# Windowed attention with an FFN behind it: global scores in the banks of the value products, and the second batch's attention in 32-query blocks

## The chip, the cores and the metric

The kernel runs on one core of one Trainium2 chip. The metric is the time of one execution on the device in microseconds (us). Every time comes from runs on the chip; the profile is that of one execution.

## The reference

Eight batches with eight heads of 64 dimensions. Each head has 512 local and 32 global tokens. A local query sees the 32 global keys and the local keys within 32 positions of it; a global query sees all 544 keys. The outputs of the heads, side by side, are the rows of x (4352 x 512), which go through an FFN:

```python
s_g = scale * q_g @ concat(k_g, k_l).T          # global queries, all keys
s_ll = where(abs(i - j) <= 32, scale * q_l @ k_l.T, -1e9)
out_l = softmax(concat(scale * q_l @ k_g.T, s_ll)) @ concat(v_g, v_l)
h = x @ w_in                                    # 512 -> 2048
out = (h - tanh(h)) @ w_out                     # 2048 -> 512
```

## The kernel before

**FFN.** x, the weights and g = h - tanh(h) are each split into a high and a low part in fp32r, and a product is three matmuls (high x high, low x high, high x low). The matmuls of the hidden layer are in line L1186, those of the output in L1234; 336 of 128x512 belong to each batch's local tokens. The 256 global tokens of all batches go through the FFN at the end (L1560 and after). The weights come as float64 and are converted on chip in 40 pieces (24 wide, 16 half). DVE takes part in all of them (L440, L444), ACT, POOL and DVE share the split into high and low (L367, L450).

**Attention.** Heads go in pairs, four pairs to a batch, 32 in all. Pairs 0 to 7 (batches 0 and 1) are of class `Pair`: 128-query tiles, in which PE turns K and Q (L544), makes scores (L640, global L577, L578), turns the probabilities (L660, L615) and multiplies with V (L737). Pairs 8 to 31 are of class `WindowPair`: 32-query blocks, in which DVE turns K and Q as they come from memory (L846, L853) and the probabilities (L1012, 16 per pair), so that PE has only scores (L873), global scores (L894) and value products (L1042). DVE takes the peaks of the rows (L972, global L906) and moves small statistics between partitions (L913, L919, which POOL may do too). The results leave a product's bank in two steps, x_hi (a cast on ACT or DVE, L367) and x_lo with the global rows xg (DVE).

**Visits.** PE's work for window pairs is grouped into visits between the FFN matmuls: both products of pair j and the scores of pair j+1 are one visit (a joint visit here); the global scores of pair j+1 are a visit of their own some FFN matmuls later, in two PSUM banks of their own. Banks 0 to 3 serve attention and the hidden layer by turns, 4 to 7 the FFN output.

**Order.** Each step is handed to a planner (`Order`) with the engines that can do it, a due time (worked out from the table `CFG`) and the data and banks that it needs. The planner lays out all engines' work in time and emits each engine's instructions in that order; each engine runs them strictly in this order. Where it expects PE to idle in the first 72 us, it puts in filler matmuls (L1842). SP issues nearly all loads, in the planned order.

Of the kernel before, what the change touches and what calls it, by code (L numbers as in the profile page):

```python
# [8 lines left out]
F32 = mybir.dt.float32  # L9
# [7 lines left out]
P = 128  # L17
D = 64
W = 32
KC = 224  # L20
KG = 352
# [186 lines left out]
def kernel(ctx, tc, q_l, k_l, v_l, q_g, k_g, v_g, w_in, w_out, out):  # L208
# [3 lines left out]
    NT = S // P  # L212
# [21 lines left out]
    wraw = [wpair[:, :256], wpair[:, 256:], cp.tile([P, 256, 2], F32, name="wraw2", tag="wraw2")]  # L234
# [19 lines left out]
    first_raw = [first_raw[:, 0], first_raw[:, 1], rawkq.rearrange("p (a t h d) -> p a t h d", a=2, t=NT, h=2)]  # L254
    first_kw = cp.tile([P, 2, 2 * S], F32, name="first_kw", tag="x_lo1")
    first_kw = [first_kw[:, 0, :2 * KG], first_kw[:, 1, :2 * KG], first_kw2]
    first_q = cp.tile([P, 4 * DM], F32, name="first_q", tag="w_out_lo4")
    wide = [wpair, first_q[:, 2 * DM:].rearrange("p (n k) -> p n k", k=2), stage[:, 0], stage[:, 1]]
    first_q = [first_q[:, :S], first_q[:, S:2 * S], cp.tile([P, S], F32, name="first_q2", tag="hi0")]
# [5 lines left out]
    SETS = [[f"{n}{u}" for n in ("rk", "rq", "pw", "pk", "pq")] for u in range(2)] + [["raw", "kq", "kw0", "kg0", "hk0"]]  # L265
# [50 lines left out]
    def bank(shape, j, dt=F32):  # L316
# [6 lines left out]
        elif len(shape) == 4:  # L323
# [4 lines left out]
    CFG = dict(win=-466.5653, a_g=1.5262, a_kg=1.4158, a_ph=0.7742, a_qs=2.9873, a_w=0.3174, a_wn=0.0, a_xg=7.3446, d_g=1.972,  # L328
               d_gl=1.6793, d_kg=0.2625, d_kq=0.1607, d_ph=0.0221, d_pl=3.1864, d_qh=27.4739, d_qs=0.035, d_tg=1.1442, d_tp=0.8276,
               d_w=0.5897, d_wl=0.2437, d_wn=2.2842, d_xg=1.1595, d_y=0.042, gfirst=0.0, ho=5649.5935, hs=-43.0719, lag=-64.2863,  # L330
               last=-56.3309, o_st0=-2045.5745, o_st1=933.0264, o_tw0=-2840.8346, o_tw1=5048.3316, one=0.0, p0=190.4904, pen=23.1854,
               penp=47.4685, s_g=0.5, s_gl=20.2886, s_kq=73.0039, s_p=1.9417, s_tg=0.5596, s_w=7.2868, s_wl=12.2887, step=129.7289,
               step1=9.9947, lag0=83.3228, hs0=44.3799, tol=0.0776, xs=0.0373, xw=3.2349, o_ld0=-276.9069, o_tn0=1314.6887,
               o_sg0=1087.8972, o_tg0=246.2107, o_s0=671.959, o_sp0=362.8471, o_t0=283.5775, o_tpp0=1378.7205, o_vl0=2890.1138,
               o_vl1=-609.1368, o_pv0=2012.3724, o_pvp0=8038.7725, o_ld1=4474.6221, o_pv1=5749.1756, o_pvp1=-4996.466,
# [433 lines left out]
    def add_window_masks():  # L769
# [24 lines left out]
        for j in range(NT):  # L794
            add(("P", 1.2), mask(j), due + j, w=["gm"], res=[("wraw", 2), "ga", "gb"] if j == 0 else ())
# [532 lines left out]
    def attention(j):  # L1328
# [3 lines left out]
        if j + 1 == H // 2:  # L1332
            add_first_globals(1)
# [545 lines left out]
```

## Time and profile before

| | us |
|---|---|
| median of 3 runs | 927.95 (927.31 to 928.08) |
| profiled execution | 928.72 |
| its span in the trace | 926.9 |
| PE busy | 912.6 |
| DVE busy | 695.1 |
| ACT busy | 393.7 |
| POOL busy | 345.4 |

The span is the time from the first to the last instruction in the trace; 1.8 us of the profiled execution lie outside it. The execution has four stages. In the start (to 60 us) batch 0's attention runs and the first weights are converted. Then batch 0's FFN runs with batch 1's attention and the other weights, to the first window visit. Then follow the FFN of batches 1 to 7 with the window pairs of the next batch between, to 796 us, and the global tokens' FFN at the end. In the trace's rows a number behind a name's line is the start, then the duration; "x4" is four instructions in a row.

### The profile page before, as it was taken

The numbers are of one execution on the slowest core, as the hardware profiler recorded it, in microseconds if no ns is written. First come the engines' busy times: TensorE is split into PE (matmuls) and PEld (weight loads), VectorE is DVE, ScalarE is ACT, GpSimd is POOL, SyncE is SP. The second block draws the span as 40 slices with busy tenths as digits, with TensorE's granted clock in tenths as the row PEclk, the third lists the DMA queues.
The fourth block names the chain that finished last, engine by engine and source line by source line (L and its number), as shares of the span: only waits on it lengthen the run. The fifth ranks groups of instructions, "written<-read, shape, count | busy, mean of one in ns | idle before, by whom it ended". The sixth has DMA issues, their size and how long they took to land.

```text
span 926.9 us, 21769 instructions
## 1 busy us (share of the span) xinstructions
PE 912.6 (98%) x7838; PEld 744.7 (80%) x7838; DVE 695.1 (75%) x2244; ACT 393.7 (42%) x1145; POOL 345.4 (37%) x588
## 2 busy tenths in 40 slices
PE   7899999999999999999999999999999999999998
PEld 5677877878888888888888888888888888898986
DVE  6887757488888896868876986778776968868773
ACT  6966666434334442433334332433334342433232
POOL 3667765633432434333332443434343432110000
PEclk9989999999999999999999999999999999999999
DMA  9555343333234332332413332432322320100001
GB/s 234 137 159 180 116 136 95 82 85 64 58 76 115 65 74 52 87 82 59 80 42 83 76 68 39 109 63 58 76 57 81 73 46 1 46 1 1 0 1 69
DMA packets 248172, 70.12 MB, mean 76 GB/s; under 512 B 232704, under 2 KB 241408, under 8 KB 248064
## 3 DMA queue, kind: packets, MB, share of 16 engines
q1 hardware_dynamic: 246720, 68.21, 31.7%
q8 instruction: 62, 1.02, 0.5%
q10 hardware_dynamic: 1344, 0.52, 0.2%
q14 instruction: 46, 0.38, 0.1%
HBM read 59.77 MB, written 8.91 MB: 74 GB/s over the span
## 4 chain that ended last, share of the span: by engine, by line
PE 94%; DVE 2%; DMA 2%; POOL 1%; ACT 0%; issue 0%; SPq 0%; ACTq 0%; DVEq 0%; POOLq 0%
PE bank L1234 34%; PE bank L1186 33%; PE bank L1560 7%; PE bank L1680 6%; PE bank L1042 5%; PE bank L873 3%; PE bank L640 1%; PE bank L894 1%; PE bank L737 1%; PE bank L1586 1%; DMA rawkq<-in_k_l_dram 1%; PE bank L660 1%; PE bank L544 1%; DMA first_raw<-in_q_l_dram 0%; DMA wpair<-in_moe_w_out_dram 0%
## 5 line engine op out<-in xcount | busy, mean ns | idle before, releaser
L1203 POOL TENSOR_TENSOR glo<-t,ghi 128x512 fp32r<-128x512 f32 x112 | 145.2, 1297 | 310.1 <-PE bank L1234 201.3
L1012 DVE STREAM_TRANSPOSE keys_first<-prob 32x256 f32<-32x256 f32 x384 | 167.4, 436 | 21.9 <-POOL prob L994 15.6
L1194 ACT ACTIVATE t<-bank 128x512 f32<-128x512 f32 x112 | 66.9, 597 | 201.1 <-PE bank L1186 197.9
L1197 DVE TENSOR_TENSOR t<-bank,t 128x512 f32<-128x512 f32 x112 | 77.2, 689 | 74.2 <-ACT t L1194 72.7
L1234 PE MATMUL bank<-w_out_hi,glo 128*128 128x512 f32 x448 | 125.5, 394 | 0.0
L1234 PE MATMUL bank<-w_out_lo,ghi 128*128 128x512 f32 x448 | 124.7, 392 | 0.0
L1234 PE MATMUL bank<-w_out_hi,ghi 128*128 128x512 f32 x448 | 124.5, 392 | 0.0
L1186 PE MATMUL bank<-x_hi,w_in_hi 128*128 128x512 f32 x448 | 123.3, 397 | 0.3 <-DVE x_hi L367 0.3
L1186 PE MATMUL bank<-x_hi,w_in_lo 128*128 128x512 f32 x448 | 120.3, 391 | 0.0
L1186 PE MATMUL bank<-x_lo,w_in_hi 128*128 128x512 f32 x448 | 120.3, 390 | 0.0
L1186 PEld LDWEIGHTS bank<-x_hi,w_in_hi 128*128 128x128 f32 x448 | 82.2, 188 | 21.4 <-DVE xg L1077 2.0
L1186 PEld LDWEIGHTS bank<-x_lo,w_in_hi 128*128 128x128 f32 x448 | 84.0, 188 | 18.1 <-issue 0.2
L1186 PEld LDWEIGHTS bank<-x_hi,w_in_lo 128*128 128x128 f32 x448 | 83.8, 188 | 18.0 <-issue 0.2
L1234 PEld LDWEIGHTS bank<-w_out_lo,ghi 128*128 128x128 f32 x448 | 83.2, 188 | 18.6 <-issue 0.7
L1234 PEld LDWEIGHTS bank<-w_out_hi,glo 128*128 128x128 f32 x448 | 82.8, 188 | 19.1 <-issue 1.5
L1234 PEld LDWEIGHTS bank<-w_out_hi,ghi 128*128 128x128 f32 x448 | 83.3, 188 | 18.2 <-issue 0.5
L994 POOL TENSOR_SCALAR prob<-prob,st 128x128 f32<-128x128 f32 x192 | 67.7, 372 | 56.6 <-DVE st L987 56.6
L367 ACT CAST ghi<-t 128x512 fp32r<-128x512 f32 (+1 forms) x76 | 46.5, 612 | 98.4 <-PE bank L1234 81.1
L980 ACT ACTIVATE prob<-prob,st 128x128 f32<-128x128 f32 x192 | 74.6, 391 | 3.1 <-DVE st L972 3.0
L1042 PEld LDWEIGHTS bank<-keys_first,values 128*64 128x64 f32 x672 | 42.2, 138 | 8.5 <-DVE t L1197 2.8
L1042 PE MATMUL bank<-keys_first 128*64 128x32 f32 (+2 forms) x672 | 46.8, 228 | 0.0
L1042 PE MATMUL bank<-keys_first,values 128*64 128x32 f32 (+2 forms) x672 | 46.8, 228 | 0.0
(252 smaller groups left out, 1476.3 us busy)
## 6 DMA issues: line engine op xcount, KB each, us to landing
out_dram<-wpair SPq DMA_DIRECT2D x28, 256.0 KB, 2.1
rawkq<-in_q_l_dram SPq DMA_DIRECT2D x96, 64.0 KB, 2.3
rawkq<-in_k_l_dram SPq DMA_DIRECT2D x96, 64.0 KB, 2.3
stage<-in_moe_w_out_dram SPq DMA_DIRECT2D x6, 512.0 KB, 3.9
wpair<-in_moe_w_out_dram SPq DMA_DIRECT2D x6, 512.0 KB, 4.3
first_q<-in_moe_w_in_dram SPq DMA_DIRECT2D x6, 512.0 KB, 4.0
stage<-in_moe_w_in_dram SPq DMA_DIRECT2D x6, 512.0 KB, 3.7
values<-in_v_l_dram SPq DMA_DIRECT2D x24, 120.0 KB, 2.3
```

The costliest lines, as they stand in the source:

```text
L367: (nc.scalar.copy if e == "A" else nc.vector.tensor_copy)(dst, src)
L980: nc.scalar.activation(x, x, AF.Exp, bias=s[:, k:k + 1], scale=-1.0, accum_out=s[:, 8 + k:9 + k])
L994: nc.gpsimd.tensor_scalar(x, x, s[:, k:k + 1], 1.0, op0=ALU.mult, op1=ALU.mult)
L1012: nc.vector.transpose(view(win_kf[W * k:W * k + W], [(CH, 2), (P, NT), (1, W)], 3 * G + W * i), src)
L1042: nc.tensor.matmul(dst, win_values[h][:, window(b)], src, start=n == 0, stop=n == len(parts) - 1, skip_group_check=True)
L1186: nc.tensor.matmul(self.h[s][:, j * n:(j + 1) * n], w[:, cc, f * P:(f + 1) * P], self.x()[xi][:, cc, :n], start=part == 0 and cc == 0 and ...
L1194: nc.scalar.activation(tt_[q], self.h[s], AF.Tanh)
L1197: nc.vector.tensor_sub(tt_[q], self.h.pop(s), tt_[q])
L1203: eng[e].tensor_sub(gg[q][1], tt_[q], f32(gg[q][0]))
L1234: nc.tensor.matmul(self.acc[tt], g[:, j * self.n + tt * P:j * self.n + (tt + 1) * P], low_out(f) if wi else high_out(f), start=s == 0 and ...
L1560: nc.tensor.matmul(self.hold(tt, tags), g(), low_out(f) if wi else high_out(f), start=first and k < len(tts), stop=last and k == len(mms) - 1)
L1680: nc.tensor.matmul(dst[:, at], w, m, start=fresh and n == 1, stop=n == 6, skip_group_check=True)
```

## The change

Three things and a new table:

- Only pairs 0 to 3 are of class `Pair`; pairs 4 to 7 are window pairs like the later ones. The window masks and the loads for them come earlier (`add_window_masks` is due at batch 1).
- The global scores of pair j+1 are glued to the joint visit, behind its local scores. They have no banks of their own: they are written into columns 288 and up of the two banks that hold the products of pair j, which come free once both the product's x_lo and the global peak have read them. The first window pair's global scores still get two banks, in the visit of its scores.
- A weight buffer (`wraw[2]`) becomes a view of one that is needed for first-pair global keys; the third sets of load buffers for pairs 4 to 7 go.
- All numbers of `CFG` are new, so that the planner lays out all engines anew.

Line numbers are 1 to 2 higher after the change (L873 is L874, L894 L896, L1012 L1014, L1042 L1044, L1186 L1188, L1234 L1236); the fillers are L1839.

```diff
-    wraw = [wpair[:, :256], wpair[:, 256:], cp.tile([P, 256, 2], F32, name="wraw2", tag="wraw2")]
+    wraw = [wpair[:, :256], wpair[:, 256:], first_kw2[:, :512].rearrange("p (n k) -> p n k", k=2)]
...
-    CFG = dict(win=-466.5653, a_g=1.5262, a_kg=1.4158, a_ph=0.7742, a_qs=2.9873, a_w=0.3174, a_wn=0.0, a_xg=7.3446, d_g=1.972,
+    CFG = dict(win=-386.7662, a_g=0.1365, a_kg=4.903, a_ph=0.7671, a_qs=2.6529, a_w=0.057, a_wn=0.2074, a_xg=0.0096, d_g=0.1819,
...
-        due = base(2 * H) - 300
+        due = base(H) - 300
...
-        def global_scores(self):
+        def global_scores(self, before=None):
             names = [("sg", self.j, h) for h in range(2)]
+            self.gtoks = names if before is None else [("o", before.j, h) for h in range(2)]
...
-                t_ = self.box["g"] = [bank([P, NG_], tags[n]) for n in names]
+                t_ = self.box["g"] = [bank([P, 288 + NG_], tags[n])[:, 288:] for n in self.gtoks]
...
-                add(("D", 0.45), peak(h), due(1.5), r=[("sg", self.j, h), "gm"], w=[key(h), (st, h)], free=[(("sg", self.j, h), 1)])
+                add(("D", 0.45), peak(h), due(1.5), r=[("sg", self.j, h), "gm"], w=[key(h), (st, h)], free=[(self.gtoks[h], 1 + (self.gtoks[h][0] == "o"))])
...
-            own = [n for x in parts for n in x["names"]]
+            own = [n for x in parts for n in x["names"] if x.get("own", True)]
...
-                w=[k + (1,) for k in x] + [("xg", 2 * self.j, half), ("xg", 2 * self.j + 1, half), ("xgw", 2 * self.j)], free=[(o, 1)])
+                w=[k + (1,) for k in x] + [("xg", 2 * self.j, half), ("xg", 2 * self.j + 1, half), ("xgw", 2 * self.j)], free=[(o, 1 + (self.j + 1 < len(pairs)))])
...
-    pairs = [(Pair if j < H else WindowPair)(j) for j in range(NH // 2)]
+    pairs = [(Pair if j < H // 2 else WindowPair)(j) for j in range(NH // 2)]
...
-        if j == H:
+        if j == H // 2:
             add_window_masks()
             add_globals(p.b)
             p.add_load()
-            p.add_visit(p.at, [p.scores()])
-        p.add_visit(p.after(1.0), [p.global_scores()])
+            p.add_visit(p.at, [p.scores(), p.global_scores()])
...
-        p.add_visit(p.after(16.0), [p.product(0), p.product(1)] + ([other.scores()] if other else []))
+        p.add_visit(p.after(16.0), [p.product(0), p.product(1)] + ([other.scores(), other.global_scores(p)] if other else []))
...
-            (attention if i < 2 * H else window_attention)(i // 2)
+            (attention if i < H else window_attention)(i // 2)
```

**How the order changes.** First PE, around the global scores of a window pair. A row names the bank written, then the weights and the moving operand. Before, they stand alone between FFN output matmuls, in two banks that nothing else uses at that time:

```order
L1234 MATMUL bank_102<-w_out_hi,ghi_72 128x512
L1234 MATMUL bank_103<-w_out_hi,ghi_72 128x512
L894 MATMUL bank_99<-first_m,win_gq 32x2x64
L894 MATMUL bank_98<-first_m,win_gq 32x2x64
...
L894 MATMUL bank_98<-first_m,win_gq 32x64
L1234 MATMUL bank_104<-w_out_lo,ghi_72 128x512
```

After, they follow the local scores of the same visit, and bank_96 is the one that the second product has just filled:

```order
L1044 MATMUL bank_96<-keys_first,values 64x96
L1044 MATMUL bank_96<-keys_first 64x96
L874 MATMUL bank_98<-first_m,hi_104 32x128
L874 MATMUL bank_99<-first_m,hi_104 32x128
...
L896 MATMUL bank_97<-first_m,win_gq 32x2x64
L896 MATMUL bank_96<-first_m,win_gq 32x2x64
...
L896 MATMUL bank_96<-first_m,win_gq 32x64
L1188 MATMUL bank_98<-x_hi_105,w_in_hi 128x512 x4
```

What moved: one visit instead of two, and the global scores now stand behind the readers of the products' banks. FFN matmuls between joint visits are 92 mostly, as the kernel before had 96; in front of the first four joint visits they are 72, 120, 108 and 84.

Second, DVE around the last x_lo of batch 0 (which the first FFN matmuls wait for) after the change. Names: `first_m` and `hi` are turned K and Q of a window pair, `st` the statistics, `stage`, `wpair` and `first_q` weight buffers:

```order
L988 TENSOR_SCALAR st_91<-st_91 128x4
L989 RECIPROCAL st_91<-st_91 128x4
L847 STREAM_TRANSPOSE first_m<-rawkq 128x5x96
L848 STREAM_TRANSPOSE first_m<-rawkq 128x32
L854 STREAM_TRANSPOSE hi_104<-rawkq 128x512
L368 CAST x_hi_85<-bank_100 128x256
...
L445 SCALAR_TENSOR_TENSOR first_q<-first_q 128x512
L921 COPY st_91<-st_91 32x2 x3
L749 TENSOR_TENSOR x_lo_86<-bank_100,x_hi_85 128x256
L753 COPY xg<-bank_100 128x32
L749 TENSOR_TENSOR x_lo_86<-bank_102,x_hi_85 128x256
```

What moved: the first window pair's softmax and the second one's turns now stand ahead of the last x_lo of batch 0, where before only weight pieces and rows of `Pair` stood. On PE, 73 fillers (before 18) stand between the last product of batch 0 and the first FFN matmul.

Third, the first rows of SP, which issue the first pairs' loads. Before:

```order
L528 DMA first_raw_81<-in_k_l_dram 128x4x64
L528 DMA first_raw_81<-in_q_l_dram 128x4x64
L483 DMA wraw2_67<-in_k_g_dram 32x8x64
L483 DMA wraw2_67<-in_q_g_dram 32x8x64
L1146 DMA values_86<-in_v_l_dram 96x3x64 x2
L1148 DMA values_86<-in_v_g_dram 32x6x64
```

After:

```order
L529 DMA first_raw_80<-in_k_l_dram 128x4x64
L1148 DMA values_84<-in_v_l_dram 96x3x64 x2
L1150 DMA values_84<-in_v_g_dram 32x6x64
L529 DMA first_raw_80<-in_q_l_dram 128x4x64
L484 DMA first_kw2_63<-in_k_g_dram 32x8x64
L484 DMA first_kw2_63<-in_q_g_dram 32x8x64
```

What moved: the three loads of V stand ahead of the first Q.

## Rows read from the trace of the kernel before

**Rows 1.** The page: busy us, share of the span and instructions of each engine.

```profile
PE 912.6 (98%) x7838; PEld 744.7 (80%) x7838; DVE 695.1 (75%) x2244; ACT 393.7 (42%) x1145; POOL 345.4 (37%) x588
```

**Rows 2.** What PE waited for: us in total, times, longest.

```profile
PE bank L544 <- DMA first_raw<-in_k_l_dram: 4.1, 1, 4.1
```

**Rows 3.** Stretches: start:end, length, busy PE, PEld, DVE, ACT, POOL, clock, DMA, GB/s.

```profile
10.00:40.00 30.00, 28.05 (x299) 20.06 (x295) 27.61 (x118) 27.15 (x93) 15.63 (x29) 1.00 0.83 211
30.00:40.00 10.00, 9.41 (x103) 6.41 (x102) 9.46 (x42) 8.96 (x31) 4.89 (x10) 1.00 0.70 184
...
10.01:187.52 177.51, 172.03 (x1269) 132.45 (x1266) 127.43 (x396) 119.85 (x335) 110.70 (x165) 0.98 0.53 142
...
187.52:796.22 608.70, 608.70 (x5917) 495.53 (x5917) 477.54 (x1675) 226.61 (x724) 222.07 (x395) 1.00 0.31 67
200.00:300.00 100.00, 100.00 (x1086) 81.40 (x1086) 85.43 (x304) 38.72 (x123) 36.36 (x70) 1.00 0.34 71
```

**Rows 4.** Timeline of PE, start of the FFN: start, us, engine, line, operation.

```profile
60.18 0.94 PE L1186 MATMUL bank<-x_hi,w_in_hi 128*128 128x512 f32 x3
61.39 0.47 PE L1186 MATMUL bank<-x_hi,w_in_hi 128*128 128x512 f32 x1 [0.27 <-DVE x_hi L367]
```

**Rows 5.** Timeline of PE, first window visit, scores and global scores together.

```profile
187.52 1.13 PE L873 MATMUL bank<-first_m,hi 64*32 64x128 f32 x63 [0.73 <-DVE first_m L847]
...
188.96 1.20 PE L1234 MATMUL bank<-w_out_hi,ghi 128*128 128x512 f32 x4
```

**Rows 6.** Timeline of PE, a joint visit and the global scores behind it.

```profile
400.21 0.30 PE L1042 MATMUL bank<-keys_first,values 128*64 128x96 f32 x1
...
402.09 1.16 PE L873 MATMUL bank<-first_m,hi 64*32 64x128 f32 x64
403.18 0.50 PE L1234 MATMUL bank<-w_out_hi,glo 128*128 128x512 f32 x1
...
407.89 1.07 PE L1186 MATMUL bank<-x_hi,w_in_lo 128*128 128x512 f32 x4
408.88 0.56 PE L894 MATMUL bank<-first_m,win_gq 64*32 64x128 f32 x32
409.38 1.20 PE L1234 MATMUL bank<-w_out_hi,glo 128*128 128x512 f32 x4
410.41 0.85 PE L1234 MATMUL bank<-w_out_hi,ghi 128*128 128x512 f32 x3
```

**Rows 7.** Timeline of PE, 72 FFN matmuls without a visit, to the global tokens' FFN.

```profile
779.90 1.07 PE L1186 MATMUL bank<-x_hi,w_in_hi 128*128 128x512 f32 x4
...
796.22 1.07 PE L1586 MATMUL bank<-x_hi,w_in_hi 128*128 128x512 f32 x4
```

**Rows 8.** Groups of DVE instructions by shape: count, busy us, mean ns, idle before.

```profile
L1012 DVE STREAM_TRANSPOSE keys_first<-prob 32x256 f32<-32x256 f32 x384 | 167.4, 436 | 21.9 <-POOL prob L994 15.6
L919 DVE COPY st<-st 32x2 f32<-32x2 f32 x138 | 26.1, 189 | 2.8
L853 DVE STREAM_TRANSPOSE hi<-rawkq 128x512 f32<-128x512 f32 x24 | 16.6, 691 | 0.8 <-PE bank L640 0.8
L444 DVE SCALAR_TENSOR_TENSOR stage<-stage 128x512 int32<-128x512 int32 x12 | 10.0, 836 | 0.4
L444 DVE SCALAR_TENSOR_TENSOR wpair<-wpair 128x512 int32<-128x512 int32 x6 | 7.0, 1174 | 0.2
```

**Rows 9.** Timeline of DVE: the first softmax, the last x_hi and x_lo of batch 0.

```profile
10.01 0.39 DVE L1124 CUSTOM_DVE_ANT_0 t<-bank,mask 128x224 f32<-128x224 f32 x1 [1.95 <-PE bank L640]
...
60.83 0.41 DVE L367 CAST x_hi<-bank 128x256 fp32r<-128x256 f32 x1
61.28 0.42 DVE L748 TENSOR_TENSOR x_lo<-bank,x_hi 128x256 fp32r<-128x256 f32 x1
61.62 0.20 DVE L750 TENSOR_TENSOR xg<-bank,xg 128x32 f32<-128x32 f32 x1
```

**Rows 10.** Timeline of SP's queue: the first loads of V.

```profile
2.81 0.96 SPq L1146 DMA_DIRECT2D values<-in_v_l_dram  x2
```

More of the change, by code (lines that the diff above doesn't have):

```diff
@@ L791, in ends @@
                 nc.vector.memset(win_gmask()[W * rows:W * rows + W, W * lo:W * hi], BIG)
-        due = base(2 * H) - 300
+        due = base(H) - 300
         for j in range(NT):
-            add(("P", 1.2), mask(j), due + j, w=["gm"], res=[("wraw", 2), "ga", "gb"] if j == 0 else ())
+            add(("P", 1.2), mask(j), due + j, w=["gm"], )
         add(("D", 0.5), ends, due, w=["gm"])
@@ L813, in add_globals @@
         add(("S", 4.4), load, due, w=["raw"], xfer=0.73)
-        add(("D", 0.56), turn, due + 64.0, r=["raw"], w=[("gkq", b % 2)], res=["fm", "gl0"] if b == 2 else [])
+        add(("D", 0.56), turn, due + 64.0, r=["raw"], w=[("gkq", b % 2)], res=["fm", "gl0"] if b == 1 else [])
     class WindowPair:
@@ L824, in __init__ @@
             self.prob, self.box = win_p, {}
-            self.over = ["h00", "h01", "h10", "h11", "hg0", "hg1"] if j == H else []
+            self.over = ["h00", "h01", "h10", "h11", "hg0", "hg1"] if j == H // 2 else []
         def after(self, us):
@@ L856, in add_load @@
                 add(("S", 2.2), load(a, src), self.after(-14.0), w=[("raw", "kq")[a]], xfer=1.46)
-            add(either(160, "gk"), common, self.after(-3.0), r=[("gkq", self.b % 2)], w=["wg"], res=["fm", "gl0"] if self.j == H else [])
-            add(("D", 0.84), keys, self.after(-3.0), r=["raw"], w=["ww"], res=["fm", "gl0"] if self.j == H else [])
+            add(either(160, "gk"), common, self.after(-3.0), r=[("gkq", self.b % 2)], w=["wg"], res=["fm", "gl0"] if self.j == H // 2 else [])
+            add(("D", 0.84), keys, self.after(-3.0), r=["raw"], w=["ww"], res=["fm", "gl0"] if self.j == H // 2 else [])
             add(("D", 0.69), queries, self.after(-3.0), r=["kq"], w=["hk0"])
@@ L895, in mm @@
                                              skip_group_check=True)
-            return dict(fn=mm, d=0.45, names=names, r=["ww", "wg", ("gkq", self.b % 2)], res=[f"pg{self.u}{h}" for h in range(2)] + ["pg0", "pg1", "pl0", "pl1"] * (self.j < H + 2),
+            return dict(fn=mm, d=0.42, names=names, own=before is None, r=["ww", "wg", ("gkq", self.b % 2)], res=[f"pg{self.u}{h}" for h in range(2)] + ["pg0", "pg1", "pl0", "pl1"] * (self.j < H // 2 + 2),
                         rows=1.0, ldw=0.03, tail=0.1, mode="s")
@@ L1096, in load @@
                             nc.sync.dma_start(dst[rows + G:], bass.AP(v.tensor, v.offset + W * D * 3, [[D, W * x], [3 * W * D, n], [1, D]]))
-            add(("S", 8.0), load, self.after(10.0), w=["vh"], res=self.over + (["vh0", "vh1"] if self.j == H else []), xfer=4.2)
+            add(("S", 8.0), load, self.after(10.0), w=["vh"], res=self.over + (["vh0", "vh1"] if self.j == H // 2 else []), xfer=4.2)
     PARTS = [[(0, 0, P, (0, 160), 0), (1, 0, 96, (64, 160), 64), (0, 1, 96, (192, 288), 160), (1, 1, P, (160, 320), P)],
```

53 lines of the change are left out of this document (25 added, 28 removed).

## The prediction

> **What bounds the kernel now.** I read the page's busy shares first. TensorE (PE) is busy for 912.6 of 926.9 us, VectorE (DVE) is second with 695.1 us [rows 1]. PE waits hardly at all: its longest wait is 4.1 us for the first load [rows 2]. So time can only be won by taking work off PE, and as long as no other engine falls behind. The table by stretches [rows 3] then shows how much room DVE has. Between 187.52 and 796.22 us PE is never idle (608.70 of 608.70) and DVE works 477.54 us, 78%; in the densest part, 200 to 300, DVE works 85.43 of 100 us and still makes PE wait for nothing. In the start, 10 to 40 us, DVE works 27.61 of 30 us (92%), and in the tightest ten of them 9.46: there DVE, not PE, sets the pace. The first FFN matmul is at 60.18 and is held up by DVE's x_hi [rows 4]; the first visit of the 32-query blocks is at 187.52 [rows 5].
>
> **What PE saves: the merged visit.** A joint visit of before (products of one pair, scores of the next) takes 1.88 us for the products (400.21 to 402.09) and 1.09 for the scores (to 403.18) [rows 6]. A visit costs more than its matmuls. Two long runs give 0.2267 us per FFN matmul (72 of them from 779.90 to 796.22 [rows 7]), so 0.907 per four. The separate global scores start 0.99 us after the last four began (407.89, 408.88), 0.09 too late, take 0.50, and the first four FFN matmuls behind them take 1.03 (409.38 to 410.41), 0.12 too long: 0.71 in all [rows 6]. In the one place where before has scores and global scores back to back, the two take 1.44 together (187.52 to 188.96) [rows 5]. So a pair costs 2.97 + 0.21 + 0.71 = 3.89 before and 1.88 + 1.44 + 0.21 = 3.53 after: 0.36 us less.
>
> **What PE saves: batch 1.** From 60.18 to 187.52 PE does 420 FFN matmuls (95.2 us); of the other 32.1 us about 1 is waiting and 31.1 is pairs 4 to 7 as 128-query tiles. As window pairs they cost 4 x 3.53 = 14.1. The stretch to 796.22 checks the prices: 2268 matmuls are 514.2 us, one visit of first scores 1.65, 23 pairs at 3.89 and a last product at 2.09 make 93.2; the sum is 607.4, the trace has 608.7, so 1.3 us are unaccounted for and I carry them along. PE alone would thus save about 31.1 - 14.1 + 23 x 0.36 = 25 us. That is the ceiling, and not what I expect.
>
> **What DVE must do first.** The softmax peaks and turns of the window form lie on DVE. In the order of after, 384 FFN matmuls (72 + 120 + 108 + 84) stand before the fourth joint visit, which needs the probabilities of pair 7; from there on the visits are as far apart as in before (88 to 100 matmuls, 92 mostly). All weight conversion on DVE (24 wide and 16 half pieces) is ahead of that visit, as all of it is ahead of 187.52 in before. So I compare DVE's work up to these two points. Before: 127.43 us busy from the first softmax at 10.01 to 187.52 [rows 3], less 0.9 for the K turn of the first window pair at its end. Out, with pairs 4 to 7: 32 local peaks (0.39 each, of which the next covers some [rows 9]), their global peaks, the copies of turned K and Q, the sums, x_hi, x_lo and two hidden tiles, all by their distances from start to start, 31 us. In: 64 turns at 0.436 [rows 8] are 27.9; 9 turns of K and Q at about 0.68 [rows 8] are 6.1; 48 small copies at 0.17 (0.189 busy [rows 8]) are 8.2 (before let POOL do 60 of the like, after none); some 100 others (peaks, sums, outputs) at 0.2 are 20: 62 us. So DVE has 126.5 + 31 = 157 us to do, and it starts later: on SP the three loads of V now stand ahead of the first Q. Two of the kind take 0.96 us [rows 10], so three some 1.5, and the first softmax moves from 10.01 to 11.5.
>
> If DVE is busy for a share u of the time, the fourth joint visit starts at V = 11.5 + 157/u. What follows on PE is fixed: 2304 matmuls (522.3), 24 joint visits at 3.53 (84.7), a last product (2.1) and the 1.3 from above, 610.4 together. Before, this stage ended at 796.22, so **the change wins if V is below 185.8, that is, if u is above 0.90**. From below, u = 0.854 (the stretch 200 to 300) gives 195.3, 9.5 us lost; from above, u = 1 gives 168.5, 17.3 won, still behind the ceiling. I take 0.93, between 10 to 40 (0.92) and 30 to 40 (0.946), since these are the rows in which DVE itself is the bound, as it will be here: V = 180.3, and 5.5 us are won. DVE cannot do much better: in each joint visit it must wait for the product before x_hi, about 1 us each time.
>
> **What else moves.** In the visit the global scores write into the banks that x_hi and x_lo are read from. Their first matmul therefore waits for the readers of the first half, on DVE or ACT, and PE's FFN is queued behind it. The scores in front cover 1.09 us; x_hi and x_lo take 0.45 and 0.34 from start to start [rows 9], the small copy behind them no more than 0.20, so the first half is free about 0.9 + 1.1 = 2 us after the visit began and the global scores come at 2.97: I cost this at nothing, with up to 0.36 per visit (the whole gain) as the other end. What the kernel does here the Trainium skill demands: its page "PSUM — Partial Sum Buffer", section "PSUM bank collisions raise a hardware error", says that guarding goes by bank and quadrant and not by address, so columns 288 and up of a bank being read are no free space. By that rule the wait can't be shed, and that is the third rival below; the kernel before, with banks of their own, shows no such wait.
>
> The end of the FFN: 40 FFN matmuls instead of 88 follow the last product. This leaves 9 instead of 20 us in which DVE can do the last batch's sums and outputs, so PE may wait up to 2 us; I take 1.5. The 73 filler matmuls in front of the first FFN matmul hold PE for no more than DVE does anyway. The 36 window-mask instructions that POOL now does near the start fall in a stretch where POOL is half idle (15.63 of 30 us [rows 3]), so nothing. The sum: -5.5 + 1.5 = -4.0 on the profiled 928.72 is 924.7; the median is 0.8 below that run, so **924.0 us**.
>
> **The rivals.** (1) *DVE keeps up.* With u of 0.96 or more V is 175 or less and 11 to 17 us go: 912 to 919. For it: a quarter of DVE's work in the FFN stage is conversion that waits for DMA alone. Against: no stretch of 10 us or more shows it. Chance 0.20. (2) *DVE is the bound and costs more than PE saves*, the case on the other side: PE stands in front of the first four joint visits. It decides at u = 0.90; at 0.88, V = 189.9 and the time is 933.5; at 0.86, 937.7. For it: 0.854 is the densest share in the FFN stage, and conversion beside POOL is dear: the same kind of piece takes 0.836 us in one tile and 1.174 in another [rows 8]. The Trainium skill's page "SBUF — State Buffer", section "Who interferes with whom", has a rule for this: a DVE instruction with two SBUF inputs and a GpSimd instruction that reads SBUF block each other for the whole instruction. If the moved masks and turns made every one of the 24 wide pieces cost 1.174 instead of these two rows' mean of 0.94, DVE would have 5.5 us more, V = 186.2, and the time would be 929.8. Chance 0.20 in all. (3) *The merged visit gains nothing*, because its global scores wait 0.36 us or more for readers; 24 visits lose 8.6 us, and the time is 932.6. Against: the 1 us of cover above. Chance 0.07. (4) *The clock falls* to 1.2 GHz in the longer start, although fillers run: the mean of 0.98 from 10.01 to 187.52 [rows 3] says that it did so for some us in before. Fillers and first FFN matmuls would take twice as long, but PE then has slack ahead of DVE: 0 to 4 us, 924 to 928. Chance 0.03.
>
> **How the numbers follow.** The forecast's own case (u from 0.90 to 0.96, nothing else) has 0.50 and runs from 919 to 930. A measurement of this kernel can tell about 0.2%, 1.9 us, from no change; so faster is below 926.0 (u above 0.919) and slower above 929.8 (u below 0.899). Faster: 0.20 + 0.34 + 0.02 = 0.56; within: 0.16 + 0.01 = 0.17; slower: 0.20 + 0.07 = 0.27. Range for 8 in 10: 912 to 934, cutting off the dear half of rival 2 and the best end of rival 1.
>
> **What would show it.** DVE's busy share from its first softmax to the fourth joint visit should be 0.93, PE should wait for DVE turns in the joint visits 1 to 4 by some 8 to 12 us in sum, the first FFN matmul should come at about 70 to 74 us (DVE's work to the last x_lo of batch 0 grows by a quarter), the stage from the fourth visit to the tail should last 610 us, and each later joint visit 3.5 us with no wait in front of the global scores. A wait of some tenths there in each visit would make rival 3 true; a V above 186 makes the forecast's sign wrong; a first FFN matmul before 68 speaks for rival 1.

## The result: slower by 6 us, and what the profile after shows

The changed kernel takes 933.74 us (median of 6 runs, 932.36 to 935.36); the kernel before, on the same chip, 927.57 (6 runs, 927.12 to 928.08). The ratio is 1.0063, with a 95% interval from 1.0052 to 1.0074. 924.0 was forecast, so the sign is wrong, and the time lies at the upper end of the range. The profiled execution took 932.36 us and is the shortest of the six.

The page of the kernel after: busy us and share of each engine (as in [rows 1]), the granted clock in 40 slices, and the chain that ended last.

```profile
PE 898.8 (97%) x8115; PEld 747.6 (80%) x8115; DVE 750.9 (81%) x2471; ACT 359.5 (39%) x1080; POOL 326.6 (35%) x529
...
PEclk9898999999999999999999999999999999999999
...
PE 80%; DVE 6%; DMA 6%; SPq 2%; POOL 2%; issue 2%; ACT 1%; ACTq 0%; POOLq 0%; DVEq 0%
```

PE lost 13.8 us of busy time [rows 1], and the kernel still got slower, because PE is now idle for 32 us of the span instead of 14. Besides DVE, the chain passes through DMA and SP's queue.

The stretches, with the columns of [rows 3]: from the first softmax (11.46) to the fourth joint visit (187.54, called V in the prediction); its part from the first FFN matmul on; and the rest.

```profile
11.46:187.54 176.08, 154.85 (x1453) 122.92 (x1449) 155.21 (x506) 105.73 (x302) 98.20 (x142) 0.95 0.58 149
72.69:187.54 114.85, 104.34 (x844) 83.00 (x841) 103.72 (x317) 59.90 (x161) 62.55 (x85) 0.97 0.54 138
187.54:799.90 612.36, 611.72 (x6011) 507.73 (x6012) 503.82 (x1777) 204.26 (x684) 214.27 (x336) 1.00 0.31 67
```

DVE was busy for 155.21 us up to V, and 157 were forecast. But that is 88% of the time, not 93, and V is 187.54 instead of 180.3. Behind V little differs from the forecast: PE is idle for 0.64 of 612.36 us.

What PE waited for, longest first (us in total, times, longest):

```profile
...
PE bank L738 <- ACT pg L588: 3.7, 1, 3.7
...
PE bank L896 <- DVE xg L1081: 2.0, 2, 1.5
PE bank L1188 <- DVE x_hi L368: 1.9, 1, 1.9
...
PE bank L1236 <- POOL w_out_lo L451: 1.6, 1, 1.6
PE bank L1236 <- ACT ghi L368: 1.4, 1, 1.4
PE bank L1044 <- DVE keys_first L1014: 1.1, 2, 0.6
```

If DVE's turns were the bound, PE would wait 8 to 12 us for them in the joint visits (L1044). It waits 1.1 (and 2.0 for the rows xg, L896). The other waits lie in the first products (L738), in first matmuls of the FFN and in those that wait for a converted weight piece (w_out_lo). So PE and DVE wait in turn, which points at a third thing; the experiments below test it.

### The profile page after: what moved, and what is told of

It reads as the page before. It is cut to its first block, busy times and chain, and to the rows that moved or that the text cites. A ratio compares the mean times of both kernels' runs of the same rounds, so it can differ in the third digit from the quotient of the medians.

```text
span 930.5 us, 22503 instructions
## 1 busy us (share of the span) xinstructions
PE 898.8 (97%) x8115; PEld 747.6 (80%) x8115; DVE 750.9 (81%) x2471; ACT 359.5 (39%) x1080; POOL 326.6 (35%) x529
## 4 chain that ended last, share of the span: by engine, by line
PE 80%; DVE 6%; DMA 6%; SPq 2%; POOL 2%; issue 2%; ACT 1%; ACTq 0%; POOLq 0%; DVEq 0%
PE bank L1236 28%; PE bank L1188 28%; PE bank L1557 7%; PE bank L1677 6%; PE bank L1044 5%; DMA wpair<-in_moe_w_out_dram 3%; PE bank L874 3%; DVE keys_first L1014 2%; PE bank L896 1%; PE bank L1583 1%; DMA stage<-in_moe_w_in_dram 1%; POOL w_in_lo L451 1%; DVE t L1199 1%; DMA first_q<-in_moe_w_in_dram 1%; SPq L1095 0%
## 5 line engine op out<-in xcount | busy, mean ns | idle before, releaser
L1014 DVE STREAM_TRANSPOSE keys_first<-prob 32x256 f32<-32x256 f32 x448 | 195.2, 436 | 9.7 <-POOL prob L996 2.2
L1196 ACT ACTIVATE t<-bank 128x512 f32<-128x512 f32 x112 | 66.9, 597 | 228.6 <-PE bank L1188 224.5
L1236 PE MATMUL bank<-w_out_hi,ghi 128*128 128x512 f32 x448 | 125.1, 393 | 2.4 <-ACT ghi L368 1.4
L1236 PE MATMUL bank<-w_out_lo,ghi 128*128 128x512 f32 x448 | 124.9, 393 | 1.6 <-POOL w_out_lo L451 1.6
L1236 PE MATMUL bank<-w_out_hi,glo 128*128 128x512 f32 x448 | 123.5, 390 | 0.0
L1188 PE MATMUL bank<-x_hi,w_in_hi 128*128 128x512 f32 x448 | 120.7, 391 | 2.9 <-DVE x_hi L368 1.9
L1188 PE MATMUL bank<-x_lo,w_in_hi 128*128 128x512 f32 x448 | 121.8, 394 | 0.7 <-DVE x_lo L749 0.7
L1188 PE MATMUL bank<-x_hi,w_in_lo 128*128 128x512 f32 x448 | 120.6, 391 | 0.0
L996 POOL TENSOR_SCALAR prob<-prob,st 128x128 f32<-128x128 f32 x224 | 83.1, 389 | 60.2 <-DVE st L989 43.6
L1188 PEld LDWEIGHTS bank<-x_hi,w_in_hi 128*128 128x128 f32 x448 | 83.8, 188 | 21.1 <-ACT x_hi L368 2.3
L1188 PEld LDWEIGHTS bank<-x_lo,w_in_hi 128*128 128x128 f32 x448 | 85.2, 190 | 19.3 <-DVE x_lo L749 1.4
L1236 PEld LDWEIGHTS bank<-w_out_hi,ghi 128*128 128x128 f32 x448 | 83.0, 188 | 21.3 <-ACT ghi L368 1.9
L1188 PEld LDWEIGHTS bank<-x_hi,w_in_lo 128*128 128x128 f32 x448 | 84.8, 189 | 17.7
L1236 PEld LDWEIGHTS bank<-w_out_lo,ghi 128*128 128x128 f32 x448 | 83.1, 188 | 19.8 <-POOL w_out_lo L451 2.0
L1236 PEld LDWEIGHTS bank<-w_out_hi,glo 128*128 128x128 f32 x448 | 83.9, 188 | 17.7
L982 ACT ACTIVATE prob<-prob,st 128x128 f32<-128x128 f32 x224 | 87.3, 392 | 21.8 <-DVE st L974 21.0
L1199 DVE TENSOR_TENSOR t<-bank,t 128x512 f32<-128x512 f32 x112 | 75.1, 684 | 22.6 <-ACT t L1196 21.3
L1077 DVE TENSOR_TENSOR x_lo<-bank,x_hi 128x256 fp32r<-128x256 f32 x56 | 23.7, 424 | 48.8 <-PE bank L896 27.6
L1044 PEld LDWEIGHTS bank<-keys_first,values 128*64 128x64 f32 x784 | 49.5, 138 | 12.1 <-DVE t L1199 7.0
L1044 PE MATMUL bank<-keys_first,values 128*64 128x32 f32 (+2 forms) x784 | 55.5, 228 | 1.4 <-DVE keys_first L1014 1.1
L1044 PE MATMUL bank<-keys_first 128*64 128x32 f32 (+2 forms) x784 | 55.4, 228 | 0.0
```

The costliest lines, as they stand in the source:

```text
L982: nc.scalar.activation(x, x, AF.Exp, bias=s[:, k:k + 1], scale=-1.0, accum_out=s[:, 8 + k:9 + k])
L996: nc.gpsimd.tensor_scalar(x, x, s[:, k:k + 1], 1.0, op0=ALU.mult, op1=ALU.mult)
L1014: nc.vector.transpose(view(win_kf[W * k:W * k + W], [(CH, 2), (P, NT), (1, W)], 3 * G + W * i), src)
L1044: nc.tensor.matmul(dst, win_values[h][:, window(b)], src, start=n == 0, stop=n == len(parts) - 1, skip_group_check=True)
L1188: nc.tensor.matmul(self.h[s][:, j * n:(j + 1) * n], w[:, cc, f * P:(f + 1) * P], self.x()[xi][:, cc, :n], start=part == 0 and cc == 0 and ...
L1196: nc.scalar.activation(tt_[q], self.h[s], AF.Tanh)
```

## Where the waits come from: SP's queue

SP issues nearly all loads, one after another, each in about half a microsecond. Its queue at the start (start, us, line, the load, count):

```profile
11.19 2.20 SPq L806 DMA_DIRECT2D rawkq<-in_k_g_dram  x4
14.09 2.74 SPq L806 DMA_DIRECT2D rawkq<-in_q_g_dram  x4
...
17.91 2.78 SPq L843 DMA_DIRECT2D rawkq<-in_q_l_dram  x4
...
22.36 1.35 SPq L1148 DMA_DIRECT2D values<-in_v_l_dram  x2
23.76 0.46 SPq L1150 DMA_DIRECT2D values<-in_v_g_dram  x1
```

These twelve issues (L806 and the L843 behind it) belong to the first 32-query pair of batch 1, whose scores come at 61.1 us. In the new order they stand ahead of V of a head of the first pair (L1148, L1150). The first value product starts at 29.02 (L738). In e3 below, with these twelve issues behind the V loads, it starts at 24.00 (L739 there):

```profile
29.02 1.97 PE L738 MATMUL bank<-keys_first,values 128*64 128x160 f32 x16 [3.75 <-ACT pg L588]
```

```profile
24.00 0.53 PE L739 MATMUL bank<-keys_first,values 128*64 128x160 f32 x1
```

The profile puts the end of this wait on ACT's pg (the global probabilities), which the product does not read; the chain of waits goes through the V load instead, 4.41 us from 23.76.

The second place comes again with each 32-query pair. Such a pair issues 8 loads of K and Q (L843) and 16 of V (L1095 to L1098). SP's queue around the end of one such block of V loads:

```profile
66.65 0.37 SPq L1095 DMA_DIRECT2D values<-in_v_l_dram  x1
...
75.97 0.60 SPq L1098 DMA_DIRECT2D keys_first<-in_v_l_dram  x1
76.67 0.55 SPq L430 DMA_DIRECT2D stage<-in_moe_w_out_dram  x1
77.32 0.38 SPq L430 DMA_DIRECT2D wpair<-in_moe_w_out_dram  x1
77.75 0.43 SPq L430 DMA_DIRECT2D stage<-in_moe_w_in_dram  x1
78.27 4.39 SPq L843 DMA_DIRECT2D rawkq<-in_k_l_dram  x4
```

ACT's timeline there (start, us, line, operation, idle before):

```profile
81.00 0.70 ACT L437 ACTIVATE stage<-stage 128x512 f32<-128x512 f32 x1 [2.64 <-DMA stage<-in_moe_w_out_dram]
...
82.86 0.60 ACT L1196 ACTIVATE t<-bank 128x512 f32<-128x512 f32 x1
...
85.10 0.61 ACT L368 CAST ghi<-t 128x512 fp32r<-128x512 f32 x1
```

Three weight loads (L430) stand behind sixteen V loads that took SP from 66.65 to 76.57. The piece `stage` is issued at 76.67 and ACT can start on it at 81.00, after 2.64 us of waiting. The FFN's own t (L1196, from the hidden layer's bank) and ghi (L368, the high part of g) stand behind that on ACT; all that ACT waits for between 78 us and ghi are loads (2.64, 0.58 and 0.54 us). So PE, which is ready for the second FFN layer, waits for ghi:

```profile
72.69 0.94 PE L1188 MATMUL bank<-x_hi,w_in_hi 128*128 128x512 f32 x3
75.52 1.70 PE L1188 MATMUL bank<-x_hi,w_in_hi 128*128 128x512 f32 x5 [1.88 <-DVE x_hi L368]
...
79.80 1.91 PE L1188 MATMUL bank<-x_hi,w_in_lo 128*128 128x512 f32 x4
...
85.76 1.20 PE L1236 MATMUL bank<-w_out_hi,ghi 128*128 128x512 f32 x4 [1.44 <-ACT ghi L368]
```

At 79.80 four matmuls take 1.91 us instead of the 1.07 of [rows 7]: the clock stands at the lower of its two levels (1.2 GHz) for a while, the mean granted clock being 0.52 of full from 76.5 to 83.5 us; PE was idle for 1.88 us before 75.52. Here this cost no time: behind the slow matmuls PE still waits 1.44 us for ghi, and ghi waits for loads. In all, the first 72 FFN matmuls take 24.2 us up to the first joint visit (96.89), against 16.3 at full rate [rows 7]; for 4.0 of these 24.2 us PE is idle.

The kernel before, in the same part of the program, has fewer issues in a row (its own SP queue; L1146 and L1148 are V, L429 the weights):

```profile
102.29 2.42 SPq L1146 DMA_DIRECT2D values<-in_v_l_dram  x2
104.75 0.47 SPq L1148 DMA_DIRECT2D values<-in_v_g_dram  x1
105.26 0.95 SPq L1146 DMA_DIRECT2D values<-in_v_l_dram  x2
106.25 0.46 SPq L1148 DMA_DIRECT2D values<-in_v_g_dram  x1
106.81 0.39 SPq L429 DMA_DIRECT2D first_q<-in_moe_w_in_dram  x1
```

Six V loads for a pair instead of sixteen. From 60 to 190 us SP issued 100 DMAs before and 137 after. It was issuing for some 85 of these 130 us in after (59 before), so SP is not busy throughout either; what its blocks of issues cost is read from e3, e4 and e10 below.

## Experiments: is it the merged visit, or batch 1?

**e1: the merged visit alone.** The kernel before, with only the global scores' part of the change; its table of numbers stays.

```diff
...
-        p.add_visit(p.after(1.0), [p.global_scores()])
...
-        p.add_visit(p.after(16.0), [p.product(0), p.product(1)] + ([other.scores()] if other else []))
+        p.add_visit(p.after(16.0), [p.product(0), p.product(1)] + ([other.scores(), other.global_scores(p)] if other else []))
```

> The kernel before with one part of the change alone: the global scores join the visit of the local ones, in the banks of the value products; pairs 4 to 7 stay 128-query tiles and the table is that of before. If the merged visit gains what the steady part of the changed kernel shows (about 0.30 us a pair, 23 pairs): 7 us, so 920.5 us, with the first window visit still near 187 us. If the global scores' wait for x_hi and x_lo eats the gain: 927 us. If the merged visit is what makes the changed kernel slow: above 930 us.

Measured: 932.95 us, ratio 1.0052 (1.0037 to 1.0067), the third of the expectations. The start did not change (first window visit 186.90, before 187.52 [rows 5]); all of the loss lies behind it, 186.90 to 800.27 = 613.4 us against 608.7 [rows 3]. PE in one visit of e1 (global scores L895, FFN L1235):

```profile
358.26 0.81 PE L895 MATMUL bank<-first_m,win_gq 64*32 64x128 f32 x32
359.00 1.20 PE L1235 MATMUL bank<-w_out_lo,ghi 128*128 128x512 f32 x4
```

DVE's readers of the same banks in that visit:

```profile
357.91 0.42 DVE L1076 TENSOR_TENSOR x_lo<-bank,x_hi 128x256 fp32r<-128x256 f32 x1 [0.34 <-ACT x_hi L367]
358.25 0.20 DVE L1078 TENSOR_TENSOR xg<-bank,xg 128x32 f32<-128x32 f32 x1
```

PE in a visit of the kernel after (global scores L896):

```profile
438.28 1.16 PE L874 MATMUL bank<-first_m,hi 64*32 64x128 f32 x64
439.18 0.59 PE L896 MATMUL bank<-first_m,win_gq 64*32 64x128 f32 x32
439.70 1.19 PE L1236 MATMUL bank<-w_out_lo,ghi 128*128 128x512 f32 x4
```

DVE's x_lo of the second half there:

```profile
439.91 0.42 DVE L1077 TENSOR_TENSOR x_lo<-bank,x_hi 128x256 fp32r<-128x256 f32 x1 [1.42 <-PE bank L896]
```

In e1 the readers of the second half stand ahead of the global scores, which take 0.74 us from start to start (358.26 to 359.00); in after the second half's x_lo follows them, and they take 0.52 (439.18 to 439.70). The wait has not gone, it lies on DVE (1.42 us), where it costs nothing. In three visits of e1 it is 1.3 to 2.2 us from the first global score to the next FFN matmul, and in two of these that matmul waits for DVE's peaks (1.58 us at 491.77, by L973), which stand behind an x_lo that had to wait. Two long stretches of FFN lose some 2 and 1 us more, where PE waits for copies on ACT (L367). So rival 3 was real under the old order, and under the new order it is gone.

**e2: batch 1 alone.** The kernel after, with the global scores as visits of their own (the two lines of e1 the other way round).

> The changed kernel with the merge taken back: the global scores are visits of their own in banks of their own; batch 1 in 32-query blocks and the new table stay. If batch 1 in blocks is what costs, and the merge gains 0.30 us a pair over 27 pairs: 8 us above the changed kernel, about 942 us. If the merge costs: below 933 us.

Measured: 952.42 us, ratio 1.0271 (1.0251 to 1.0291). Both expectations failed, and it does not isolate the part: the planner also laid the start out anew (first FFN matmul 82.06, V 196.66). In the profiled execution (950.3 us span, after 930.5) V is 9.1 us later; the other 10.7 lie behind V and fit 24 visits at 0.43, which is what the merge saves per pair in the new order (some 3.94 us a pair with the global scores apart, 3.51 together). So how the 6 us divide between the merged visit and batch 1 is not settled; in the late part the merge gains.

**e5: merge with the new order for the late part only.** e1 with the late half (`L_...`) of the new table.

> The kernel before with the merged visit (as in the run with the merge alone), and of the new table only the half that holds from batch 3 on; batch 1 stays in 128-query tiles, the start keeps the old table. In the merge-only run the global scores took 0.74 us in nearly all visits (0.50 alone) and five visits lost 1 to 2 us more; in the changed kernel's late part they take 0.52. If this is the old order's doing (x_hi and x_lo come too late under it): 0.52 in the late visits, 20 pairs gain 0.43 us each, and the time is 917 to 920 us. If the wait lies in the merge itself: as the merge alone, 930 to 933 us.

Measured: 1092.22 us, ratio 1.1759. The two halves of different tables give a bad plan; the run says nothing on the merge.

## Experiments: SP's queue or DVE's work?

**e3: first V loads first.** Only SP's order changes: the twelve window loads go behind the V loads of the first pair (a delay on these issues when the order is written out, 10 or 16 us for the twelve and 0 for all others).

```diff
-            out.append((s, o.seq, o.fn, e, o.args))
+            out.append((s + o.behind, o.seq, o.fn, e, o.args))
```

> The changed kernel with one thing moved on SP: the 12 issues of the first window pair's loads (global K and Q, local Q) in the start stand behind the V loads of the first pair instead of ahead of them; all other engines keep their order. If SP's queue holds up the start: PE's first value product comes at about 25 us instead of 29.0, DVE's idle of 4.9 us there goes, and the first FFN matmul and the fourth joint visit come 3 to 5 us earlier, 929 to 931 us. If DVE's work alone sets the pace: no change in the fourth joint visit (187.5 us) and in the time, 933 to 934 us.

Measured: 929.2 us, ratio 1.0022 (1.0008 to 1.0036). The first product starts at 24.00, V is 186.11, and the first expectation held.

**e4: weight loads on ACT's queue.** The 38 loads of L430 are issued by ACT, at the same places of the plan.

```diff
-                nc.sync.dma_start(raw.bitcast(I32)..., src)
+                nc.scalar.dma_start(raw.bitcast(I32)..., src)
```

> The changed kernel with the 38 weight loads issued from ACT's queue instead of SP's, at the same places of the planned order; nothing else differs. If SP's queue (140 issues from 60 to 190 us, against 102 before) holds up the weight pieces: DVE's waits for weight DMAs (4.6 us) and PE's for weights (3 us) go, and the time falls by 3 to 6 us, to 928 to 931 us. If DVE's work alone sets the pace: no gain, and ACT's 38 issues of 0.5 us may cost some us, 934 to 940 us.

Measured: 929.14 us, ratio 1.0025 (1.0006 to 1.0043); V is 183.98, and the first expectation held. The weight piece of the place above reaches ACT sooner (L437 at 79.01 instead of 81.00), and the second FFN layer starts 10.0 us after the first FFN matmul (74.29) instead of 13.1:

```profile
84.30 1.20 PE L1236 MATMUL bank<-w_out_hi,ghi 128*128 128x512 f32 x4 [1.03 <-ACT ghi L368]
```

The wait for ghi itself is hardly shorter than in after (1.03, was 1.44), because PE, which runs at full clock there, also comes sooner.

**e6: both.**

> The changed kernel with both moves on SP's queue: the first pair's V loads ahead of the window pair's, and the 38 weight loads on ACT's queue. Each alone gave about 4.5 us. If they take away two different hold-ups: 924 to 926 us, and the fourth joint visit at 181 to 183 us. If both only shift what DVE's work then limits: 928 to 930 us.

Measured: 927.8 us, ratio 0.9992 (0.9975 to 1.0009); V is 184.78. Two moves of DMA issues, with no other work added or taken away, take back the 6 us: as fast as the kernel before, and no faster. The gains nearly add up (0.41% and 0.38% alone, 0.71% together); the time lies between the two expectations, and V above the 181 to 183 of the first.

**e7: less work for DVE.** In 12 of the wide weight pieces DVE joins the two parts on 64 of 512 columns only (the other columns of these weights are left unjoined).

```diff
+            if kind == "o" and not half:
+                v, up = v[:, :64], up[:, :64]
             nc.vector.scalar_tensor_tensor(v, up, 3, v, ...)
```

> The changed kernel with 9 us of DVE work left out before the fourth joint visit: in 12 of the 24 wide weight pieces the joining of the two words (0.8 to 1.2 us each) is done on an eighth of the columns, so these weights are not the reference's; order, loads and waits stay. If DVE's work sets the pace to the fourth joint visit (rival 2): it comes 7 to 10 us earlier, and the time is 924 to 927 us. If SP's queue and the loads set it: less than 4 us, 930 to 934 us.

Measured: 932.17 us, ratio 1.0048 (1.0028 to 1.0068). The stretch up to V in e7, with the columns of [rows 3]:

```profile
11.46:187.54 176.08, 154.57 (x1454) 124.07 (x1452) 147.62 (x507) 106.04 (x303) 97.69 (x142) 0.94 0.58 150
```

One group of DVE's part of the conversion there, with the columns of [rows 8] (the last: idle before, and what ended it; in after this group waited 1.4 us for its loads):

```profile
L441 DVE TENSOR_SCALAR stage<-stage 128x512 int32<-128x512 int32 x12 | 6.4, 532 | 3.5 <-DMA stage<-in_moe_w_out_dram 3.4
```

DVE is busy for 7.6 us less (147.62 against 155.21; some 4.3 of them are the shortened joins) and V does not move (187.47). What DVE no longer did, it waited. By the prediction's formula V would have moved by 7.6 / 0.93 = 8 us. This is the run that takes the prediction's picture down: of the kernels in the table below e7 has the least DVE time up to V, and its V is that of after. That time is no fixed amount of work, either. The same 506 instructions of DVE up to V (give or take two) took 155.2 us in after, 152.8 in e3, 150.0 in e4 and 149.2 in e6, which change nothing on DVE.

**e9: e6 and e7 together.** With the queue out of the way, is DVE the bound then?

> The kernel after with both moves of e6 (first V loads ahead of the window loads, weight loads on ACT), and with the DVE work of e7 left out: in 12 of the wide weight pieces DVE joins the two parts on an eighth of the columns only, so these weights are wrong in the rest, and some 7.6 us of DVE's work ahead of the fourth joint visit are gone. In e7 that work was taken away with SP's queue as it was, and the visit stayed at 187.5. Theory A, DVE is the bound as soon as SP's queue no longer starves it (the prediction's picture, only hidden in after): the visit falls by 4 to 7 us against e6's 184.8, and the time is 921 to 924. Theory B, loads and the weight chain remain the bound: the visit stays within 1.5 us of 184.8, and the time is 926 to 929.

Measured: 928.95 us, ratio 1.0009 (0.9992 to 1.0025); V is 184.4, e6 184.78: theory B's time and V. But the run does not answer its question, since DVE's busy time up to 184.4 did not fall (149.75 us, e6 148.80). The joins of stage and wpair took 5.4 us less there, but others of the same 506 instructions took longer, the 48 small copies of the statistics above all (15.1 us, e6 11.9).

**e10: more issues, same work.** The opposite of e3 and e4: each large V load of the pairs of batch 1 is cut into three, 48 more issues on SP, the same bytes, the same order.

```diff
-                        nc.sync.dma_start(dst[:rows], bass.AP(v.tensor, ...))
+                        cut = [0, rows // 3, 2 * rows // 3, rows] if self.b == 1 else [0, rows]
+                        for lo, hi in zip(cut, cut[1:]):
+                            nc.sync.dma_start(dst[lo:hi], bass.AP(v.tensor, ... + D * lo, ...))
```

> The kernel after, with the large V load of each head and third of the four window pairs of batch 1 cut into three DMAs by rows: the same bytes and the same work, in the same order, but 12 more issues on SP for each of these pairs, 48 in all, some 24 us more at the 0.5 us that an issue takes there. Theory, SP's in-order queue starves the start: the weight loads behind these issues come later, the fourth joint visit moves from 187.5 to 191 or more, and the time is 937 to 945. Rival, the queue is not what sets the pace (the transfers, the conversion chain or the clock do): the visit stays within 1 us of 187.5 and the time is 932 to 935.

Measured: 946.28 us, ratio 1.0198 (1.0183 to 1.0213); V is 200.91, 13.4 later. The same places as shown above for after, now in e10. SP's queue from the block's first V load to the weight load behind it:

```profile
67.33 2.82 SPq L1097 DMA_DIRECT2D values<-in_v_l_dram  x3
...
81.58 0.55 SPq L430 DMA_DIRECT2D stage<-in_moe_w_out_dram  x1
```

ACT's conversion of that piece, and the FFN's t behind it:

```profile
85.20 0.68 ACT L437 ACTIVATE stage<-stage 128x512 f32<-128x512 f32 x1 [6.63 <-DMA stage<-in_moe_w_out_dram]
...
87.16 0.58 ACT L1198 ACTIVATE t<-bank 128x512 f32<-128x512 f32 x1
```

PE's first matmul of the second FFN layer:

```profile
90.01 2.07 PE L1238 MATMUL bank<-w_out_hi,ghi 128*128 128x512 f32 x4 [7.30 <-ACT ghi L368]
```

The block is 4.2 us longer (67.33 to 81.58 instead of 66.65 to 76.67), the weight piece is issued 4.9 us later, ACT starts on it 4.2 us later, and PE waits 7.30 us for ghi instead of 1.44. The bytes and the order are the same, and the weight piece is with ACT no later behind its own issue than in after (3.6 us, was 4.3). So SP's queue sets the pace here. V and the time moved further than the theory had put them.

**e11: e10 with the weight loads on ACT.**

> The same cut V loads as in e10, with the weight loads issued by ACT (as in e4). Theory, the queue harms by way of the weight loads that stand behind other issues: with these out of it the 48 more issues cost little, the visit stays near e4's 184.0, and the time is 929 to 932. Rival, the queue harms by way of K, Q and V of the window pairs themselves: the visit moves as far as in e10, by 3 us or more, and the time is 933 to 940.

Measured: 944.78 us, ratio 1.0162 (1.0128 to 1.0196). The first three visits come 1.5 to 4 us later than in after (98.37, 131.54, 163.58; after 96.89, 129.90, 159.82), not 6 to 14 as in e10 (102.78, 138.35, 174.13), but the fourth is as late as there (200.36). So the theory, which put V near 184, failed. PE and DVE now wait for the pairs' own loads. PE's longest wait in e11 between 10 and 215 us (us in total, times, longest):

```profile
PE bank L1044 <- DMA keys_first<-in_v_l_dram: 9.3, 3, 4.1
```

DVE's longest, between 10 and 195 us:

```profile
DVE first_m L811 <- DMA rawkq<-in_k_g_dram: 8.3, 1, 8.3
```

These loads are late because SP stands still between its issues, as here, where it waits 6.8 us:

```profile
103.45 1.58 SPq L1098 DMA_DIRECT2D values<-in_v_g_dram  x1
111.89 0.32 SPq L1100 DMA_DIRECT2D values<-in_v_l_dram  x1
```

By the profile SP waits there until a weight load that ACT issued has landed. From 60 to 202 us such waits in front of K and V loads come to 54.2 us in e11 (16 times), 17.2 in e4, 18.2 in e6, 0.6 in after and none in e10. Why they come with the weights on a second queue no run shows. So e11 does not tell whether the longer queue by itself would have made K and V late.

**e8: V loads on ACT as well.** e6, with the 16 V loads of each window pair issued by ACT.

> The kernel after with three moves of DMA issues and nothing else: the window loads behind the first pair's V loads on SP (as in e3), the weight loads issued by ACT (as in e4), and in addition the 16 V loads of each window pair issued by ACT too, so that SP issues little but K, Q and the global parts. Theory, SP's queue is what starves the start: with the V loads gone from it too, the first pairs' V and K loads run as early as their buffers allow; the fourth joint visit falls from 184.8 (e6) to about 182, and the time is 924 to 926. Rival, e6 has already taken all that the queue held up and the rest is the chain load, conversion, free buffer, and DVE's own work: 927 to 929. Third: ACT, which is in order too, waits with a V load for its buffer and holds the exponentials behind it: the joint visits wait for ACT, and the time is 930 to 936.

Measured: 1202.86 us, ratio 1.2953. The third expectation had the direction, but put the loss at 3 to 9 us above the kernel before; it is 275.6. ACT in one visit (start, us, line, idle before):

```profile
401.28 0.32 ACTq L1098 DMA_DIRECT2D values<-in_v_l_dram  x1
...
410.13 0.60 ACTq L1101 DMA_DIRECT2D keys_first<-in_v_l_dram  x1
410.78 0.37 ACT L369 CAST x_hi<-bank 128x256 fp32r<-128x256 f32 x1 [9.78 <-DMA keys_first<-in_v_l_dram]
```

Between the x_hi of the two halves (the first at 400.63) ACT issues sixteen loads, 9.5 us, and the global scores on PE wait for the second x_hi: 170.3 us in 20 visits (`L899 <- ACT x_hi`). Here an issue on ACT's queue cost about 0.6 us of ACT.

## Why the prediction was wrong, point by point

**V sets the time, as the prediction said.** The profiled time less V is nearly the same in all kernels with the new order:

| kernel | V | time of that execution | difference |
|---|---|---|---|
| forecast | 180.3 | 924.7 | 744.4 |
| after | 187.54 | 932.36 | 744.8 |
| e3 | 186.11 | 931.45 | 745.3 |
| e4 | 183.98 | 930.16 | 746.2 |
| e6 | 184.78 | 929.63 | 744.9 |
| e7 | 187.47 | 931.71 | 744.2 |
| e9 | 184.39 | 929.56 | 745.2 |
| e10 | 200.91 | 947.53 | 746.6 |
| e11 | 200.36 | 946.38 | 746.0 |

A V is that of one execution, and the runs of e3, e4, e6 and e9 lie 5 to 10 us apart, so between these kernels a difference of 1 or 2 us in V says nothing.

The part behind V held in its sum, partly by luck. V to 799.90 took 612.36 us where 610.4 were forecast, and at the end, where 1.5 us of waiting had been put, PE waits for nothing; the two nearly cancel. A joint visit takes 3.51 us (products 1.88, scores 0.90, global scores 0.52, and 0.21), where 3.53 were forecast; the early ones, between 212 and 286 us, wait some tenths for readers (0.79 instead of 0.52). The break-even of V was put at 185.8, which leaves out the 1.5 us of the end; by the differences of the table it is 183.9 (928.72 - 744.8). e6 at 184.78 took 929.63 in that execution, after at 187.54 is slower.

**The step that failed is u.** DVE's start (11.5; 11.46) was right, the first FFN matmul (70 to 74; 72.69) too. DVE's work (157 us; 155.2 measured) came out in its sum, but two of its terms missed in opposite ways: the 48 small copies took 0.327 us each where the row that they were priced by has 0.189 (15.7 us in all instead of 9.1), and the joins of the wide weight pieces took 18.0 us instead of the 22.1 of before. That the sum fits is partly luck. The share of time in which DVE can work was taken from rows in which it *was* the bound in the kernel before [rows 3], and it was assumed that it would be the bound again. It was 0.88, because DVE had to wait and not because it could do no more. e7 shows it by taking work away without effect, e3, e4 and e6 by moving DMA issues with an effect, e10 by lengthening the queue. A share of busy time is a result, and can't be carried over as if it were a property of the engine.

**What was left out is SP's queue.** The prediction counted three issues on SP, V ahead of the first Q, and found them at 1.5 us. It did not count the twelve issues of the first window pair ahead of the remaining V loads (e3: 0.4% of the time), nor that each pair of batch 1 as a window pair issues 24 DMAs of half a microsecond, behind which weight loads stand (e4: 0.4%). Both could be counted in the two orders.

**The rivals.** Rival 2 has the time (its 0.88 gives 933.5) but not the reason: that DVE's work is the bound in after is refuted by e7. Its dear case, in which each wide piece costs the 1.174 us of one row, did not come true: the join of wpair took 0.709 us on average where before has 1.174 [rows 8], stage 0.709 where before has 0.836. How much of such differences is the blocking that the Trainium skill's page "SBUF — State Buffer", section "Who interferes with whom", states no run here shows.

Rival 3 is true in e1 and not in after. In the visit of after shown above, the second half's x_lo starts at 439.91, behind the end of the global scores (439.18 + 0.59). This agrees with the rule named there, from the Trainium skill's page "PSUM — Partial Sum Buffer", section "PSUM bank collisions raise a hardware error", by which guarding goes by bank and quadrant and not by address. But the rule leaves open which of the two waits, and in after it is DVE.

Rival 4 came in part: the mean granted clock up to V is 0.95, where before had 0.98 [rows 3]. In the first 72 FFN matmuls the low clock cost nothing, as shown above. For the whole start it is open: in e3, e4 and e6 the half of the runs with the lower mean clock took 2.3 to 3.1 us longer than the other half, and no run shows whether the clock makes them longer or longer waits of PE the clock lower. In e4 PE waited in that stretch nearly as long as in after (3.7 us, 4.0) at full clock, so such waits alone do not decide it.

**What stays open.** e6 has V at 184.78, still 4.5 us behind the forecast. There DVE waits 5.0 us once for a K load (L849, until 53.08) and some 2 us each for scores, exponentials and products; SP stands still for 18.2 us until weight loads of ACT have landed; PE's mean clock is between 0.70 and 0.84 of full in each ten us from 30 to 60. Which of these would have to go first for the forecast's 924, and whether DVE would then be the bound, was not settled. No kernel was found that is clearly faster than the one before.

## What to carry to other kernels

Before a bound is set by an engine's work, count what each queue issues per unit of work, in both forms of the work: here a 128-query pair loads V with 6 DMAs and a 32-query pair with 16, half a microsecond each, and the weights stood behind them. When a stage has no single busy engine, test the rate by taking work off the supposed bound and by shortening and lengthening the supposed queue; what has the effect sets the pace. Read first whether the run did take the work off (e7 against e9). Moving issues to ACT's queue helped with 38 issues in the start (e4), and held up ACT's casts with 16 for every pair (e8).

## What the runs showed of the hardware

In after a DMA issue holds SP for 0.33 to 0.6 us mostly, whether the load has 32 or 512 KB, and for over 1 us now and then (four K loads: 4.39 us). Cutting loads of the same bytes into three cost 13.4 us at V for 48 issues, 0.28 us each. ACT pays about the same: 16 issues in 9.5 us (e8).

The join of a wide weight piece on DVE (128x512) took between 0.71 and 1.17 us on average, by tile and kernel, without a change in its shape. In e7, where half of `stage`'s joins were shortened to 64 columns, the other half took 0.909 us on average instead of 0.709, so some of the saved work came back. The small copies of the statistics (32x2) took 0.327 us on average up to V in after and 0.248 in e6, where before has 0.189 over the whole kernel for one of its two groups [rows 8].

The kernels with moved issues scatter more from run to run: e6 lay between 924.92 and 933.06 us (10 runs), the kernel before, on the same chip, between 927.00 and 930.64 (14 runs). Why was not shown.
